# A gated recurrence feeding a mixture of experts on one core: another order table, and masks ahead of one state

## The chip, the core and the metric

The kernel runs on one core of a Trainium2 chip. Its engines are TensorE (PE; PEld is its weight load), VectorE (DVE), ScalarE (ACT), GpSimd (POOL) and SyncE (SP), which here only issues DMAs. Each engine works through its own list of instructions strictly in order and waits at an instruction until what that instruction needs is there. The metric is the device time of one execution in microseconds (us), as the median of several runs.

## The reference, cut to what matters

Four batches of eight heads, 768 steps, head size 48. A complex gate `a` of magnitude at most 0.999 drives a 48 x 48 state per head:

```
S = a[t] * S + k[t] v[t]^T        (complex; a scales the rows)
y[t] = q[t] . real(S)
x = y as 3072 tokens of 384
e = argmax(x @ w_gate);  g = softmax(x @ w_gate)[e]
out = g * relu(x @ w1[e]) @ w2[e]     (8 experts, 1024 wide, capacity 768)
```

## The kernel before, in words

**Tiling of the recurrence.** The 768 steps are cut into 8 chunks of 96. Inside a chunk the answer is an attention matrix with a triangular mask, and between chunks a state is handed on. What both need are the running products of the gate inside a chunk. VectorE computes these step by step (the scan, `scan_ops`, tiles `xy` and `near`) for two groups of two batches: group 0 is batches 0 and 1, group 1 is batches 2 and 3. Each group is done in seven pieces. For each piece a gate part runs ahead (`norm_ops`: tiles `a`, `xp`, `lnn`, `c0n`, `t5n`) and a product part behind (`post_ops`: tiles `qkin`, `wp`, `v0`, `qko`), at whose end GpSimd stores the scaled q and k to a scratch tensor in DRAM: the first 8 rows of each chunk to `scr0_0` or `scr1_0`, the other 88 to `scr0_1` or `scr1_1` (group 0 or 1).

**Units.** A unit is one batch and one chunk, named (batch, chunk). There are 32; the first 16 go (0,0), (1,0), (0,1), (1,1) up to (1,7), then (2,0) opens group 1. A unit (`Att.unit`) loads its part of the scratch (`qkc`, three buffers) and its values (`v`, three buffers), both issued by SyncE; TensorE turns q and k (`tr`), ScalarE copies them out (`qT`, `kT`); TensorE multiplies them in two halves (`pa`, one PSUM buffer in the first 14 units); VectorE masks each half into `a_sb`; TensorE forms the output (`y`). TensorE also forms the chunk's own state (`s`, one PSUM buffer shared with `y`), VectorE adds the state handed over (`s`), SyncE swaps its real and imaginary rows by two DMAs (`sx`), and the next state `z` comes from `u` (scaled `s`) and the scaled `sx`. The last chunk of a batch hands nothing on. ScalarE copies `y` to `xt`, TensorE turns it (`x`), and the router starts from that.

**What sets the order.** In slots, one per unit, each step has a place: the lists `SLOT`, `SLOT_A`, `SLOT_B` give the steps of a slot in order, each with the distance of the unit that it belongs to. `M0` and `M1` are the two masks, `D` is the state's sum and its swapping transfer, `U`, `ZA` and `ZB` make the next state, `A0` and `A1` are the two products, `T0` to `T3` the turns. `SLOT_A` is used for slot 13 alone. The slots up to 12 are mixed with the scan of group 1 into one list of 740 steps, and the table `ORDER` of 740 numbers says in which order these steps are issued on all of the engines. That part, from about 122 to 250 us, is called the stretch here; its table ends with the work of unit (0,6), the 13th. Behind it come slot 13 and the slots after it, in the order of their lists. After the last unit the expert part follows, with TensorE at work to the end.

The places that matter below: the transfer of a state is `swap` (L603 and L604), the mask is `cut` (L578), the state's three steps are L615, L620 and L625, the scratch loads are `load_qk` (L552), the value loads `load_v` (L555), the scratch stores L489 and L494, the turns L563, the two products L574.

Of the kernel before, what the change touches and what calls it, by code (L numbers as in the profile page):

```python
# [49 lines left out]
SLOT_A = SLOT[:-1] + [("LS", 3), SLOT[-1]]  # L50
SLOT_A.insert(SLOT_A.index(("D", 0)), ("LB", 3))
SLOT_A.remove(("L", 3))
SLOT_0 = SLOT[:1] + [("L", 2)] + SLOT[1:]
SLOT_B = [("S", 0), ("L", 3), ("R2", -3), ("G", -3), ("M0", -1), ("T1", 1), ("M1", -1), ("R3", -3), ("P", -3), ("W", -3),
          ("F", -2), ("X", -2), ("E", -2), ("D", 0), ("R1", -2), ("A0", 0), ("ZA", -1), ("T2", 1), ("Y", -1), ("T0", 1), ("A1", 0),
# [15 lines left out]
for j in SIDE:  # L71
# [5 lines left out]

ALONE = 14
ORDER = [
# [31 lines left out]
]  # L111
CAP = 0.9990000128746033

# [19 lines left out]
class Att:  # L133
# [520 lines left out]
    def slots(self):  # L654
# [8 lines left out]
        for n in range(-2, len(us) + 3):  # L663
            for i, (t, o) in enumerate(SLOT_0 if n == -2 else SLOT if n < ALONE - 1 else SLOT_A if n < ALONE else SLOT_D if n == len(us) - 2 else SLOT_B):
                if 0 <= n + o < len(us) and (t, o, n) != ("M0", -1, ALONE):
# [971 lines left out]
```

## Time and profile before

| what | value |
|---|---|
| median of 3 runs | 628.46 us (626.43 to 633.83) |
| the profiled execution's own time | 631.67 us |
| its span, first to last instruction | 630.0 us |
| PE, DVE, ACT, POOL busy | 87%, 70%, 55%, 33% of the span |
| mean granted TensorE clock | 0.951 |

The busy shares of the page are means over stages with different limits, so the stages are shown one by one below. Times in the rows are counted from the span's start. A row of the order of time gives the start, the duration, the line, what it writes and reads, how many instructions were merged in it, and in brackets how long the engine stood idle before it and what ended that. A granted clock of 1.00 is 2.4 GHz, 0.50 is 1.2 GHz.

### The profile page before, as it was taken

The numbers are of one execution on the slowest core, as the hardware profiler recorded it, in microseconds if no ns is written. First come the engines' busy times: TensorE is split into PE (matmuls) and PEld (weight loads), VectorE is DVE, ScalarE is ACT, GpSimd is POOL, SyncE is SP. The second block draws the span as 40 slices with busy tenths as digits, with TensorE's granted clock in tenths as the row PEclk, the third lists the DMA queues.
The fourth block names the chain that finished last, engine by engine and source line by source line (L and its number), as shares of the span: only waits on it lengthen the run. The fifth ranks groups of instructions, "written<-read, shape, count | busy, mean of one in ns | idle before, by whom it ended". The sixth has DMA issues, their size and how long they took to land.

```text
span 630.0 us, 12176 instructions
## 1 busy us (share of the span) xinstructions
PE 547.1 (87%) x4295; PEld 476.9 (76%) x4295; DVE 441.0 (70%) x1266; ACT 345.6 (55%) x771; POOL 207.7 (33%) x212
## 2 busy tenths in 40 slices
PE   0767656569899999799999998999999999999996
PEld 0333323247688889699889997998999999999995
DVE  5989999988999997249459786265555564556551
ACT  7777757787888785355454552243435353435440
POOL 9476863248878701004232221001010102020112
PEclk9887888688999999799999997999999999999999
DMA  6195858769888769568888821744546453636301
GB/s 201 51 295 207 274 187 286 247 208 230 256 251 234 192 204 260 149 141 227 216 207 212 212 76 48 238 120 131 163 121 178 132 168 119 179 114 188 107 27 49
DMA packets 73398, 111.88 MB, mean 178 GB/s; under 512 B 6568, under 2 KB 63214, under 8 KB 72048
## 3 DMA queue, kind: packets, MB, share of 16 engines
q1 hardware_dynamic: 66384, 77.13, 45.2%
q0 software_dynamic: 6944, 33.88, 15.3%
q8 instruction: 36, 0.59, 0.4%
q14 instruction: 34, 0.28, 0.1%
HBM read 72.99 MB, written 34.21 MB: 170 GB/s over the span
## 4 chain that ended last, share of the span: by engine, by line
PE 59%; DMA 10%; DVE 5%; ACT 4%; issue 1%; SPq 1%; POOLq 0%; POOL 0%; DVEq 0%; ACTq 0%
PE ph L1231 17%; PE my L1239 15%; PE pa L574 4%; PE tr L563 4%; PE s L587 4%; PE y L635 2%; PE x L844 2%; PE my L1253 2%; PE y L640 2%; DMA raw<-in_moe_w_dram 2%; PE wp L210 2%; PE yt L1193 1%; DMA qkc<-scr 1%; DMA scr<-qko 1%; DMA v<-in_v_dram 1%; PE mt L1167 1%
## 5 line engine op out<-in xcount | busy, mean ns | idle before, releaser
L1204 POOL DMA_INDIRECT out_dram<-o,xr x26 | 25.2, 969 | 156.7 <-DVE o L1203 139.9
L1277 ACT ACTIVATE hh<-ph 128x448 fp32r<-128x448 f32 (+5 forms) x64 | 33.0, 516 | 78.2 <-PE ph L1231 78.1
L1278 DVE SCALAR_TENSOR_TENSOR hl<-ph,hh 128x448 fp32r<-128x448 f32 (+5 forms) x64 | 37.3, 583 | 50.5 <-ACT hh L1277 49.1
L867 POOL DMA_INDIRECT disp<-x,idx x32 | 30.7, 960 | 119.3 <-DVE sl L929 41.9
L1129 DVE TENSOR_TENSOR lo<-raw,hi 128x384 fp32r<-128x384 f32 (+2 forms) x128 | 66.0, 551 | 3.2 <-ACT hi L1126 3.2
L210 PE MATMUL wp<-qko,ident 128*128 128x384 f32 x92 | 43.4, 623 | 27.3 <-ACT qko L408 23.5
L563 PE MATMUL tr<-ident,qkc 96*96 96x96 f32 x512 | 63.5, 252 | 3.8 <-DMA qkc<-scr 3.2
L574 PE MATMUL pa<-qT,kT 128*96 128x96 f32 x512 | 56.9, 255 | 5.8 <-DVE a_sb L578 5.5
L1126 ACT CAST hi<-raw 128x384 fp32r<-128x384 f32 (+2 forms) x128 | 60.0, 515 | 0.0
L1239 PE MATMUL my<-hh,lo 128*128 128x448 f32 (+5 forms) x168 | 59.6, 355 | 0.0
L1239 PE MATMUL my<-hl,hi 128*128 128x448 f32 (+5 forms) x168 | 59.2, 352 | 0.0
L210 PE MATMUL xp<-a,ident 128*128 128x384 f32 x84 | 37.8, 591 | 23.6 <-ACT a L238 23.1
L574 PEld LDWEIGHTS pa<-qT,kT 128*96 128x96 f32 x512 | 50.4, 170 | 8.5 <-DVE a_sb L578 5.9
L563 PEld LDWEIGHTS tr<-ident,qkc 96*96 96x96 f32 x512 | 47.8, 129 | 10.1 <-issue 4.1
L210 PEld LDWEIGHTS wp<-qko,ident 128*128 128x128 f32 x92 | 21.0, 241 | 45.2 <-ACT qko L408 31.8
L1239 PE MATMUL my<-hh,hi 128*128 128x448 f32 (+5 forms) x168 | 54.2, 355 | 0.0
L1231 PE MATMUL ph<-xh,hi 128*128 128x448 f32 (+5 forms) x192 | 49.9, 362 | 0.0
L336 DVE TENSOR_TENSOR xy<-a,near 128x192 f32<-128x192 f32 x135 | 47.4, 351 | 3.2
L1231 PE MATMUL ph<-xl,hi 128*128 128x448 f32 (+5 forms) x192 | 48.9, 354 | 0.0
L367 DVE TENSOR_REDUCE near<-xy 128x96 f32<-128x192 f32 x129 | 45.9, 356 | 4.3 <-ACT a L377 1.2
L568 ACT COPY qT<-tr 96x384 f32<-96x384 f32 x64 | 30.4, 476 | 32.0 <-PE tr L563 24.9
L210 PEld LDWEIGHTS xp<-a,ident 128*128 128x128 f32 x84 | 18.5, 231 | 38.3 <-issue 23.2
(220 smaller groups left out, 1362.3 us busy)
## 6 DMA issues: line engine op xcount, KB each, us to landing
raw<-in_moe_w_dram SPq DMA_DIRECT2D x64, 384.0 KB
qkc<-scr SPq DMA_DIRECT2D x32, 528.0 KB
scr<-qko POOLq DMA_DIRECT2D x10, 1536.0 KB
disp<-fill POOLq DMA_DIRECT2D x7, 772.0 KB
v<-in_v_dram SPq DMA_DIRECT2D x32, 144.0 KB
xr<-disp SPq DMA_DIRECT2D x6, 675.5 KB
sx<-s SPq DMA_DIRECT2D x56, 72.0 KB
a<-in_a_re_dram SPq DMA_DIRECT2D x10, 384.0 KB
```

Of the source, the lines that this page charges most:

```text
L210: nc.tensor.matmul(out=pt[:, :m], lhsT=self.ident, rhs=t[:, h:h + m], start=i == 0, stop=i == 1)
L336: nc.vector.tensor_tensor(out=xy, in0=crossed(a4[:, s, 1, cs]), in1=w, op=ALU.mult)
L367: nc.vector.tensor_reduce(out=o, in_=xy.rearrange("p z d -> p (z d)").rearrange("p (u d z) -> p u d z", u=2, z=2)[:, :, cs], op=ALU.add, a ...
L563: nc.tensor.transpose(out=pt[:, h * C:h * C + C], in_=qk(slice(0, C), 4 * hh + h, slice(z_ * C, z_ * C + C)), identity=self.ident[:C, :C])
L574: nc.tensor.matmul(out=pa[:, h * C:h * C + C], lhsT=kT[:, 4 * hh + h], rhs=qT[:, 4 * hh + h], start=True, stop=True)
L867: ins = nc.gpsimd.indirect_dma_start(out=self.disp, out_offset=bass.IndirectOffsetOnAxis(ap=idx[:, c:c + 1], axis=0), in_=x[:, c, :], in_o ...
L1126: nc.scalar.copy(out=hi[i][:, s], in_=raw[i][:, s])
L1129: nc.vector.tensor_tensor(out=lo[i][:, s], in0=raw[i][:, s], in1=hi[i][:, s].bitcast(F32), op=ALU.subtract)
L1231: nc.tensor.matmul(out=ph[:, :WIDTHS[e]], lhsT=a[:, k, fs], rhs=r[:, k, :WIDTHS[e]], start=k == 0 and i == 0, stop=k == KT - 1 and i == 2)
L1239: nc.tensor.matmul(out=py[m][:, :WIDTHS[e]], lhsT=a[:, f % self.PF, ms], rhs=r[:, :WIDTHS[e]], start=f == 0 and i == 0, stop=f == NF - 1 a ...
L1277: nc.scalar.activation(hh[:, :w], ph[:, :w], AF.Relu)
L1278: nc.vector.scalar_tensor_tensor(out=hl[:, :w], in0=ph[:, :w], scalar=0.0, in1=hh[:, :w].bitcast(F32), op0=ALU.max, op1=ALU.subtract)
```

## The change

The table `ORDER` is replaced by another one with the same 740 steps: some 170 of them stand elsewhere in the stretch, and near its end the transfer of the last state in it, that of unit (0,6), comes at an earlier place in SyncE's list. In `SLOT_A` the two steps `ZA` and `ZB` (of unit (0,6)) move behind the mask `M0` (of unit (1,6)). No instruction is added or removed.

```diff
 SLOT_A.remove(("L", 3))
+SLOT_A = [x for x in SLOT_A if x[0] not in ("ZA", "ZB")]
+for x in (("ZB", -1), ("ZA", -1)):
+    SLOT_A.insert(SLOT_A.index(("M0", 0)) + 1, x)
 SLOT_0 = SLOT[:1] + [("L", 2)] + SLOT[1:]
...
 ORDER = [
-    1, 0, 2, 6, 4, 9, 7, 5, 12, 11, 13, 14, 10, 17, 19, 3, 15, 21, 20, 29, 18, 23, 28, 36, 39, 104, 30, 26, 62, 27,
...
-    715, 719, 723, 729, 647, 732, 731, 726, 727, 735, 730, 733, 739, 712, 720, 734, 721, 728, 722,
+    1, 10, 0, 2, 6, 4, 9, 62, 5, 11, 104, 13, 3, 7, 14, 19, 21, 15, 23, 12, 17, 28, 29, 20, 18, 36, 39, 40, 8, 26, 27,
...
+    710, 717, 718, 726, 725, 729, 720, 732, 733, 681, 722, 727, 735, 730, 739, 728, 712, 731, 734,
 ]
```

In the lists below a line number of the kernel after the change is 3 higher than before. **SyncE at the end of the stretch**, first before, then with the change. The tiles are `sx_b_c` (swapped state of a unit), `v` and `qkc` (the three buffers each of values and scratch); `qkc0` is for unit (1,7), `qkc1` from `scr1` for unit (2,0).

```order
L603 DMA sx_1_5_2593<-s_1_5_2592 48x384
L604 DMA sx_1_5_2593<-s_1_5_2592 48x384
L555 DMA v1_106<-in_v_dram 96x384
L555 DMA v2_107<-in_v_dram 96x384
L552 DMA qkc0_102<-scr0_1_95 88x8x192
L552 DMA qkc0_102<-scr0_0_94 8x8x192
L603 DMA sx_0_6_2723<-s_0_6_2722 48x384
L604 DMA sx_0_6_2723<-s_0_6_2722 48x384
L552 DMA qkc1_103<-scr1_1_97 88x8x192
L603 DMA sx_1_6_2831<-s_1_6_2830 48x384
```

```order
L606 DMA sx_1_5_2569<-s_1_5_2568 48x384
L607 DMA sx_1_5_2569<-s_1_5_2568 48x384
L555 DMA qkc2_104<-scr0_1_95 88x8x192
L555 DMA qkc2_104<-scr0_0_94 8x8x192
L558 DMA v1_106<-in_v_dram 96x384
L606 DMA sx_0_6_2705<-s_0_6_2704 48x384
L607 DMA sx_0_6_2705<-s_0_6_2704 48x384
L558 DMA v2_107<-in_v_dram 96x384
L555 DMA qkc0_102<-scr0_1_95 88x8x192
L555 DMA qkc0_102<-scr0_0_94 8x8x192
L555 DMA qkc1_103<-scr1_1_97 88x8x192
L606 DMA sx_1_6_2831<-s_1_6_2830 48x384
```

The two DMAs of `sx_0_6` stood behind the load of `v2` and both loads of `qkc0`, and now stand ahead of them. The stores move too, on **GpSimd's queue at the same place**, before and with the change:

```order
L481 TENSOR_TENSOR qko_1_4_2089<-a4_1_4_1373,v0_1_4_2118 128x16x96
L489 DMA scr1_1_97<-qko_1_4_2089 128x3072
L620 TENSOR_TENSOR sx_1_3_2125<-sx_1_3_2125,pcol0_100 96x384
L625 TENSOR_TENSOR z2_117<-u_1_3_2238,sx_1_3_2125 96x384
L494 DMA scr1_0_96<-qko_1_6_2499 64x1536 x2
L489 DMA scr1_1_97<-qko_1_5_2363 128x3072
```

```order
L623 TENSOR_TENSOR sx_1_3_2126<-sx_1_3_2126,pcol0_100 96x384
L628 TENSOR_TENSOR z2_117<-u_1_3_2228,sx_1_3_2126 96x384
L484 TENSOR_TENSOR qko_1_4_2096<-a4_1_4_1355,v0_1_4_2131 128x16x96
L492 DMA scr1_1_97<-qko_1_4_2096 128x3072
L492 DMA scr1_1_97<-qko_1_5_2362 128x3072
L497 DMA scr1_0_96<-qko_1_6_2533 64x1536 x2
```

The store of `qko_1_5` now stands ahead of the two of `qko_1_6`, where it stood behind them. On VectorE the product that completes `qko_1_6` (L439 before) moves behind the sum of `s_0_6`, so these two stores come after it.

**VectorE behind the stretch**, slot 13 and the start of slot 14, before and with the change (`a_sb1` are the masked halves of unit (1,6), `sx_0_6`, `z1` and `u` belong to the states):

```order
L578 TENSOR_TENSOR a_sb0_113<-pa_0_6_1_2775,mask_81 96x384
L599 TENSOR_TENSOR s_1_6_2830<-s_1_6_2806,z2_117 96x384
L620 TENSOR_TENSOR sx_0_6_2723<-sx_0_6_2723,pcol0_100 96x384
L625 TENSOR_TENSOR z1_116<-u_0_6_2741,sx_0_6_2723 96x384
L578 TENSOR_TENSOR a_sb1_114<-pa_1_6_0_2837,mask_81 96x384
L615 TENSOR_TENSOR u_1_6_2874<-s_1_6_2830,pcol0_100 96x384
L578 TENSOR_TENSOR a_sb1_114<-pa_1_6_1_2882,mask_81 96x384
L620 TENSOR_TENSOR sx_1_6_2831<-sx_1_6_2831,pcol0_100 96x384
```

```order
L581 TENSOR_TENSOR a_sb0_113<-pa_0_6_1_2779,mask_81 96x384
L602 TENSOR_TENSOR s_1_6_2830<-s_1_6_2806,z2_117 96x384
L581 TENSOR_TENSOR a_sb1_114<-pa_1_6_0_2835,mask_81 96x384
L623 TENSOR_TENSOR sx_0_6_2705<-sx_0_6_2705,pcol0_100 96x384
L628 TENSOR_TENSOR z1_116<-u_0_6_2777,sx_0_6_2705 96x384
L618 TENSOR_TENSOR u_1_6_2874<-s_1_6_2830,pcol0_100 96x384
L581 TENSOR_TENSOR a_sb1_114<-pa_1_6_1_2882,mask_81 96x384
L623 TENSOR_TENSOR sx_1_6_2831<-sx_1_6_2831,pcol0_100 96x384
```

The first mask of unit (1,6) stood behind `sx_0_6` and `z1`, which wait for the transfer, and now stands ahead of them; the second mask stays behind.

**SyncE in the first part of the stretch**, before and with the change (`qkc0`, `qkc1`, `qkc2` for units (0,0), (1,0), (0,1); `qkin_1_1` are q and k for the second piece of group 1, `a_1_4` the gate of its fifth):

```order
L552 DMA qkc0_102<-scr0_1_95 88x8x192
L552 DMA qkc0_102<-scr0_0_94 8x8x192
L396 DMA qkin_1_1_1109<-in_q_dram 128x768
L397 DMA qkin_1_1_1109<-in_k_dram 128x768
L552 DMA qkc1_103<-scr0_1_95 88x8x192
L552 DMA qkc1_103<-scr0_0_94 8x8x192
L603 DMA sx_0_0_1232<-s_0_0_1231 48x384
L604 DMA sx_0_0_1232<-s_0_0_1231 48x384
L552 DMA qkc2_104<-scr0_1_95 88x8x192
L552 DMA qkc2_104<-scr0_0_94 8x8x192
L228 DMA a_1_4_1312<-in_a_re_dram 128x768
L229 DMA a_1_4_1312<-in_a_im_dram 128x768
```

```order
L555 DMA qkc0_102<-scr0_1_95 88x8x192
L555 DMA qkc0_102<-scr0_0_94 8x8x192
L555 DMA qkc1_103<-scr0_1_95 88x8x192
L555 DMA qkc1_103<-scr0_0_94 8x8x192
L399 DMA qkin_1_1_1132<-in_q_dram 128x768
L400 DMA qkin_1_1_1132<-in_k_dram 128x768
L555 DMA qkc2_104<-scr0_1_95 88x8x192
L555 DMA qkc2_104<-scr0_0_94 8x8x192
L606 DMA sx_0_0_1227<-s_0_0_1226 48x384
L607 DMA sx_0_0_1227<-s_0_0_1226 48x384
L558 DMA v2_107<-in_v_dram 96x384
L231 DMA a_1_4_1281<-in_a_re_dram 128x768
```

The loads of `qkc1` stand ahead of `qkin_1_1`, and those of `qkc2` ahead of the transfer `sx_0_0`, which waits for the first unit's state.

## Rows read from the trace of the kernel before

**Rows 1.** Stages of core 0: length, busy PE, PEld, DVE, ACT, POOL, PEclk, DMA, GB/s

```profile
140.67:145.67 5.00, 5.00 (x41) 5.00 (x41) 4.80 (x14) 4.70 (x9) 3.51 (x2) 0.66 0.65 153
170.00:226.00 56.00, 54.01 (x599) 45.92 (x597) 52.80 (x153) 44.92 (x109) 39.88 (x30) 1.00 0.82 235
226.00:255.00 29.00, 28.64 (x375) 26.44 (x372) 21.85 (x43) 18.38 (x57) 2.20 (x4) 1.00 0.78 210
259.26:264.73 5.47, 5.47 (x33) 5.22 (x33) 2.52 (x5) 1.03 (x3) 0.00 (x0) 0.50 0.51 133
```

**Rows 2.** TensorE in order of time, 251 to 268: start, us, line [idle before]

```profile
251.09 0.88 PE L844 MATMUL x<-wx,xt 112*96 112x104 f32 x8
...
251.80 0.84 PE L574 MATMUL pa<-qT,kT 128*96 128x96 f32 x8
...
252.48 0.49 PE L563 MATMUL tr<-ident,qkc 96*96 96x96 f32 x4
...
254.38 0.87 PE L563 MATMUL tr<-ident,qkc 96*96 96x96 f32 x8
...
259.26 1.59 PE L574 MATMUL pa<-qT,kT 128*96 128x96 f32 x8 [4.01 <-DVE a_sb L578]
...
267.38 0.82 PE L563 MATMUL tr<-ident,qkc 96*96 96x96 f32 x8
```

**Rows 3.** VectorE in order of time, 238 to 259

```profile
238.43 0.95 DVE L439 TENSOR_TENSOR qko<-a,qkin 128x768 f32<-128x768 f32 x1
...
244.53 0.54 DVE L599 TENSOR_TENSOR s<-s,z 96x384 f32<-96x384 f32 x1
...
246.80 0.56 DVE L620 TENSOR_TENSOR sx<-sx,pcol 96x384 f32<-96x384 f32 x1 [0.16 <-DMA sx<-s]
...
257.59 0.55 DVE L620 TENSOR_TENSOR sx<-sx,pcol 96x384 f32<-96x384 f32 x1 [6.08 <-DMA sx<-s]
...
258.65 0.55 DVE L578 TENSOR_TENSOR a_sb<-pa,mask 96x384 f32<-96x384 f32 x1
```

**Rows 4.** SyncE's DMA issues in order of time, 239 to 254

```profile
239.21 0.58 SPq L604 DMA_DIRECT2D sx<-s  x1
...
240.20 8.20 SPq L555 DMA_DIRECT2D v<-in_v_dram  x2
...
248.45 2.53 SPq L552 DMA_DIRECT2D qkc<-scr  x2
...
251.08 0.98 SPq L603 DMA_DIRECT2D sx<-s  x1
...
253.89 0.29 SPq L552 DMA_DIRECT2D qkc<-scr  x1
```

**Rows 5.** GpSimd's DMA issues in order of time, 241 to 244

```profile
241.60 1.12 POOL L494 DMA_DIRECT2D scr<-qko  x2 [22.38 <-DVE qko L481]
243.27 0.55 POOL L489 DMA_DIRECT2D scr<-qko  x1 [0.55 <-DVE psq L518]
```

**Rows 6.** Chain that ended last, in order of time: start, us, what

```profile
123.00 8.31 DMA scr<-qko
...
131.33 2.36 DMA qkc<-scr
...
190.93 6.50 DMA qkc<-scr
```

**Rows 7.** TensorE in order of time, at 140

```profile
140.67 0.84 PE L563 MATMUL tr<-ident,qkc 96*96 96x96 f32 x8 [1.90 <-DMA qkc<-scr]
```

**Rows 8.** VectorE in order of time, 137 to 149

```profile
137.01 0.36 DVE L367 TENSOR_REDUCE near<-xy 128x96 f32<-128x192 f32 x1 [1.21 <-ACT a L377]
...
148.41 0.57 DVE L448 TENSOR_TENSOR wp<-wp,v 128x384 f32<-128x384 f32 x1 [1.67 <-ACT v L430]
```

**Rows 9.** ScalarE in order of time, at 139

```profile
139.49 0.46 ACT L597 COPY s<-s 96x384 f32<-96x384 f32 x1
```

**Rows 10.** SyncE's DMA issues in order of time, at 132

```profile
132.59 0.88 SPq L552 DMA_DIRECT2D qkc<-scr  x2
```

58 rows, old and new, of the table ORDER are left out of this document.

## The prediction, on record before the change was run

> **What bounds the kernel now.** I read the views in this order: the table of stages, TensorE's and VectorE's order of time where a stage has idle time, then the issues of SyncE and GpSimd that these waits lead to.
>
> The stages [rows 1] show two different limits. From 170 to 226 us TensorE is busy 54.01 of 56.00 us and VectorE 52.80: nothing can be moved there to gain much. From 226 to 255 TensorE has 28.64 of 29.00, VectorE only 21.85: TensorE bounds, and VectorE has slack. Right behind, TensorE stands still for 4.01 us, from 255.25 to 259.26, for a mask `a_sb`, and its clock is then at 0.50 (1.2 GHz, against 2.4 GHz before the idle time) for 5.47 us [rows 1, 2]. After 265 it is at work again with only small gaps, into the expert part; so what is saved at 255 should reach the end.
>
> Why the mask is late is in VectorE's rows [rows 3]. It had stood idle for 6.08 us at the product `sx` at 257.59, waiting for a transfer; the mask of 258.65 is two instructions behind, though its input, the product `pa` of 251.80 + 0.84 = 252.64 [rows 2], had long been there. And the transfer is late because of SyncE [rows 4]: the state that it carries was complete at 244.53 + 0.54 = 245.07 [rows 3], but SyncE stood 8.20 us at the `v` loads of 240.20, then issued `qkc` from 248.45, and the transfer's second DMA only at 252.10. It landed 5.5 us later. A wait of VectorE, ended by a DMA that was queued 6 us after its data existed, is what the edit takes aim at.
>
> **The end of the stretch, step by step.** (1) The transfer. Its earlier place lets it go at about 245.1. The one before it took from 239.21 [rows 4] to 246.80 [rows 3], 7.6 us, the late one 257.59 - 251.08 = 6.5. So it lands at 251.6 to 252.7. The mask cannot start before 252.64, so the transfer is no longer what VectorE waits for. (2) The mask ahead of `sx` and `z1`. With the transfer at 245.1 this makes little difference by itself; it takes the mask out of the transfer's reach should that be late. `sx`, `z1` and `u` behind it cost 0.59, 0.47 and 0.47 start to start, so the second mask is free to go at 255, before TensorE asks for it. (3) TensorE then goes on at 255.25, the full 4.01 us earlier. (4) With no idle time I expect the clock to stay at 1.00: 5.47 us of work at half the clock is 2.74 at the full one, a further 2.74. Together 6.75.
>
> What may be given back. SyncE now stands at the transfer until 245.1, with `v2`, `qkc0` and `qkc1` queued behind. In the trace `v2` was held to 248.4 anyway by the buffer that it needs, so the transfer's early place costs them nothing as long as the sum of `s_0_6` comes before that. `qkc0`, still issued from 248.45, is wanted one product after 255.25, at 255.25 + 0.68 = 255.93 (0.68 is the start-to-start of `pa`, 251.80 to 252.48). Loads of this kind took 2.36 and 6.50 us [rows 6] and 140.67 - 132.59 = 8.08 [rows 7, 10]: it lands between 250.8 and 256.5, a wait of 0 to 0.6. `qkc1` needs the stores of GpSimd. The last product of `qko_1_6` (0.95, as at 238.43 [rows 3]) now follows the sum of `s_0_6`: 245.07 + 0.95, and 0.3 to the issue, is 246.3, against 241.60 before [rows 5]. A store took 8.31 [rows 6], and the one of 243.27 had landed when SyncE issued the load behind it, at 253.89 [rows 4, 5], 10.6 later. So the store lands at 254.6 to 256.9, the small load behind it at 257.0 to 263.4. TensorE wants it halfway through the turns of 267.38 [rows 2], at 267.82 - 6.75 = 261.07: a wait of 0 to 2.3. Both together 0 to 2.9. I take 0.6, since three of the four corners of the second give nothing or next to it. **End: 6.75 - 0.6 = 6.1.**
>
> **The first part of the stretch.** The other places of the table touch three waits. The copy of `near` by ScalarE held VectorE 1.21 us at 137.01, and the copy of `v` 1.67 at 148.41 [rows 8]. The load of unit (1,0) held TensorE 1.90 us at 140.67 [rows 7], and its clock over the next 5.00 us averaged 0.66 [rows 1], 1.70 lost. The load now goes ahead of two others, and ScalarE's copy is asked for earlier. But ScalarE's copy of `s_0_0` (139.49 to 139.95 [rows 9]) comes about 0.7 later, since two more small copies stand ahead of it, and the next state's product on TensorE needs the buffer that it frees. So TensorE's wait shrinks from 1.90 to perhaps 1.2 rather than to nothing, and the 1.21 of VectorE goes.
>
> What reaches 226 is the smaller of the two engines' gains, since both are nearly full from 170 on. Upper end: VectorE's 1.21 + 1.67 = 2.9 (TensorE's would be 3.6). Lower end: the other table could open one new wait of the size of the largest that VectorE had here, -1.7. The totals of work are the same, and I find as many pairs of neighbouring VectorE instructions of the scan that depend on each other as before. I take **1.5**, half of the upper end, since one of the two waits of VectorE is clearly addressed and the other is not.
>
> **Sum.** 6.1 + 1.5 = 7.6 on the profiled execution's own 631.67 (span 630.0 and 1.67 around it): 624.1. This execution is 3.2 above the median of 628.46, inside the spread of the three runs. Nothing in the terms hangs on that, so I take 7.6 off the median: **620.9**.
>
> **A rule that speaks against step (1).** In the trace a transfer that was issued at 239.21 was seen complete by 246.80, before the stores of 241.60 and 243.27 had landed, and the late one of 251.08 was seen after them. Neither shows what a transfer does that is issued between such stores. The Trainium skill, "DMA: Bandwidth & Descriptors", section "Queues, rings and completion order", says that a transfer's completion signal lands only after every earlier write from the same DMA engine, across its queues. By it a transfer issued among stores would be seen only when these are through. The sum would then be 7.1 instead of 7.6, for the reason given in rival R, whose numbers come from the rows.
>
> **The rivals.**
> - **A, the end alone.** The stretch gains nothing, its places cancel. For it: from 170 on both engines are full, and ScalarE's copy of `s_0_0` comes later. 628.46 - 6.1 = 622.4. Chance 0.17.
> - **B, the wait moves on.** The end gives back its upper 2.9 at the loads `qkc0` and `qkc1`, and the stretch gains nothing: 6.75 - 2.9 = 3.85, or 624.6; with the clock falling again after that wait it could be 627. For it: the store goes 4.7 us later than before. Against: half of the combinations of flights leave no wait. Chance 0.13.
> - **R, the transfer is seen with the stores.** If it lands at 256.9, the first mask is safe by its new place, but the second goes at 256.9 + 0.59 + 0.47 + 0.47 = 258.4 and ends at 259.0. TensorE wants it for `y` at 255.25 + 0.68 + 0.44 + 0.71 + 0.68 + 0.44 = 258.2, so it waits 0.5 to 0.8: 7.6 - 0.5 = 7.1, or 621.4. Chance 0.06.
> - **C, slower: the sum of `s_0_6` comes late.** SyncE stands at the transfer, and `v2`, both `qkc0` and `qkc1` queue behind; the stores of `qko_1_6` wait behind the same sum. It decides at about 247: a sum later than that by x shifts the store and the load by x. With 3 us, which a stretch that reads worse on VectorE would bring, the load lands at up to 266.4 against 261.07: 5.3 of waiting and again some 2.7 of clock, 8.0 lost beside the 6.75 gained, and the 3 us of the stretch itself: 628.46 + 8.0 - 6.75 + 3 = 632.7; between 630 and 636. For it: 170 steps in a stretch with no slack. Against: the sum is as many instructions from the end of VectorE's list as before. Chance 0.12.
> - **D, no effect.** The transfer is held by something that I don't see, and the first mask's new place alone only moves TensorE's wait from the first mask to the second: 627 to 629. Chance 0.09.
>
> **The numbers.** My forecast has 0.43, its own range 618 to 622.3. A difference of 1% of the median, 6.3 us, is about what a measurement of this kernel can tell from no change: below 622.2 is faster, above 634.7 slower. Faster: 0.38 of the forecast, 0.07 of A, 0.05 of R, 0.50. Slower: some 0.07, half of C and what it stands for. The rest, 0.43, is within 1%. The range goes from 617 (6.75 + 2.9 and 2 for the spread of the medians) to 629, with C and a tail of each side left out.
>
> **What would show it.** Right: no wait of TensorE over 1 us between 254 and 266, granted clock 1.00 there; the transfer's DMAs issued within 1 us of the sum of `s_0_6`; the wait of 137.01 gone. Wrong: a wait of TensorE at a `tr` near 256 or 261 ended by `qkc` (B); the second mask waiting at `sx` (R or D); the sum of `s_0_6` later than 247 (C); a stage 134 to 226 that is no shorter (A).

## The result, and the profile after

The change makes the kernel faster: 629.3 us before, 623.7 with it (medians of 20 runs each), ratio 0.9914 with a 95% interval of 0.9889 to 0.9939, which is 5.4 us less (3.8 to 7.0). The profiled execution has a span of 625.5 us against 630.0, 4.5 less. The kernel with both end edits and the new first part, tested below, was profiled in one of its slow runs (631.46 us, the median of its fast ones is 624.84), so its pieces stand in no comparison. (The table has 728 numbers for its 740 steps; the same 12 are left out before and after. By a plain count 692 of the 728 stand at another place in it, 191 of them by ten places or more, where "some 170" was said above. Line numbers with the change are 3 higher.)

TensorE with the change, in order of time (start, duration, line, what; in brackets the idle time before and what ended it):

```profile
255.87 0.87 PE L566 MATMUL tr<-ident,qkc 96*96 96x96 f32 x8
256.57 0.84 PE L577 MATMUL pa<-qT,kT 128*96 128x96 f32 x8
258.11 0.51 PE L566 MATMUL tr<-ident,qkc 96*96 96x96 f32 x4 [0.69 <-DMA qkc<-scr]
...
262.80 0.84 PE L566 MATMUL tr<-ident,qkc 96*96 96x96 f32 x8
```

These answer to the rows from 254.38 on in [rows 2]. The product `pa` follows the turns without a wait; the 4.01 us are gone. From these turns to the ones that were at 267.38 it is 262.80 - 255.87 = 6.93 us now, and was 267.38 - 254.38 = 13.00: 6.07 less. What is left is a wait of 0.69 for the load of unit (1,7). The stage has its full clock (length, then busy PE, PEld, DVE, ACT, POOL, the granted clock, DMA share, GB/s):

```profile
256.57:263.64 7.07, 6.37 (x86) 5.77 (x84) 1.96 (x4) 3.40 (x9) 0.00 (x0) 1.00 0.77 207
```

VectorE there with the change, beside [rows 3]:

```profile
245.78 0.55 DVE L602 TENSOR_TENSOR s<-s,z 96x384 f32<-96x384 f32 x1
...
254.17 0.55 DVE L581 TENSOR_TENSOR a_sb<-pa,mask 96x384 f32<-96x384 f32 x1 [1.17 <-PE pa L577]
254.65 0.54 DVE L623 TENSOR_TENSOR sx<-sx,pcol 96x384 f32<-96x384 f32 x1
...
257.45 0.55 DVE L581 TENSOR_TENSOR a_sb<-pa,mask 96x384 f32<-96x384 f32 x1 [1.20 <-PE pa L577]
```

The mask now waits for its own input, and `sx` behind it no longer waits at all. SyncE's issues, beside [rows 4], show why:

```profile
238.81 2.29 SPq L555 DMA_DIRECT2D qkc<-scr  x2
241.93 0.33 SPq L558 DMA_DIRECT2D v<-in_v_dram  x1
246.36 0.52 SPq L606 DMA_DIRECT2D sx<-s  x1
246.93 0.65 SPq L607 DMA_DIRECT2D sx<-s  x1
249.29 0.34 SPq L558 DMA_DIRECT2D v<-in_v_dram  x1
249.68 3.04 SPq L555 DMA_DIRECT2D qkc<-scr  x3
```

The transfer goes 0.03 us after the sum is complete (245.78 + 0.55 = 246.33), where it went 6 us after it before. The second `v` behind it still goes at about the same point, when its buffer is free.

But the sum itself is 1.25 us later than in [rows 3], and the end of the stretch with it (the turns of 255.87 by 1.49). The reason lies ahead of the change. The first product of the stretch, which both kernels reach through the same work, opens 3.08 us later in this execution, at 131.26 against 128.18; with both counted from there, the turns at the end come after 124.61 us with the change and 126.20 before, 1.59 less. TensorE in the first part of the stretch with the change:

```profile
131.26 2.90 PE L213 MATMUL wp<-qko,ident 128*128 128x384 f32 x4 [4.07 <-DVE t5n L278]
...
140.39 0.89 PE L577 MATMUL pa<-qT,kT 128*96 128x96 f32 x8 [0.66 <-ACT qT L571]
...
142.81 1.60 PE L590 MATMUL s<-v,qkc 128*96 128x96 f32 x16 [0.87 <-ACT s L600]
...
250.84 1.57 PE L590 MATMUL s<-v,qkc 128*96 128x96 f32 x16 [0.40 <-DMA v<-in_v_dram]
```

The wait of 1.90 for the load [rows 7] is gone, and 0.66 + 0.87 took its place, the second of them at `s` behind ScalarE's copy. A new wait of 0.40 for `v` stands at 250.84.

So this pair of traces alone would say: 6.1 at the end, 1.6 in the stretch, 7.7 together, less 3.1 by the chance of a later opening. One execution each is thin for a difference of 1.6, and that was the first thing to test.

### The profile page after: what moved, and what is told of

It reads as the page before. It is cut to its first block, busy times and chain, and to the rows that moved or that the text cites. A ratio compares the mean times of both kernels' runs of the same rounds, so it can differ in the third digit from the quotient of the medians.

```text
span 625.5 us, 12179 instructions
## 1 busy us (share of the span) xinstructions
PE 544.3 (87%) x4295; PEld 473.1 (76%) x4295; DVE 440.9 (70%) x1266; ACT 344.0 (55%) x771; POOL 208.0 (33%) x212
## 4 chain that ended last, share of the span: by engine, by line
PE 67%; DVE 11%; ACT 9%; DMA 9%; issue 2%; SPq 1%; POOLq 0%; POOL 0%; DVEq 0%; ACTq 0%
PE ph L1234 18%; PE my L1242 15%; PE wp L213 5%; PE tr L566 4%; PE pa L577 4%; PE s L590 4%; DMA v<-in_v_dram 4%; PE x L847 3%; PE y L638 2%; DVE xy L339 2%; PE xp L213 2%; PE my L1256 2%; PE y L643 2%; DMA qkc<-scr 2%; DMA a<-in_a_im_dram 2%
## 5 line engine op out<-in xcount | busy, mean ns | idle before, releaser
L213 PE MATMUL wp<-qko,ident 128*128 128x384 f32 x92 | 46.8, 661 | 27.9 <-ACT qko L411 22.9
L566 PE MATMUL tr<-ident,qkc 96*96 96x96 f32 x512 | 61.9, 248 | 2.3 <-DMA qkc<-scr 0.9
L577 PE MATMUL pa<-qT,kT 128*96 128x96 f32 x512 | 54.6, 249 | 2.2 <-ACT qT L571 1.3
L577 PEld LDWEIGHTS pa<-qT,kT 128*96 128x96 f32 x512 | 48.9, 164 | 4.6 <-issue 1.1
L590 PE MATMUL s<-v,qkc 128*96 128x96 f32 x448 | 43.3, 249 | 5.4 <-DMA v<-in_v_dram 4.1
L1234 PE MATMUL ph<-xh,lo 128*128 128x448 f32 (+5 forms) x192 | 47.1, 353 | 0.0
```

Source lines behind the costliest of these rows:

```text
L213: nc.tensor.matmul(out=pt[:, :m], lhsT=self.ident, rhs=t[:, h:h + m], start=i == 0, stop=i == 1)
L566: nc.tensor.transpose(out=pt[:, h * C:h * C + C], in_=qk(slice(0, C), 4 * hh + h, slice(z_ * C, z_ * C + C)), identity=self.ident[:C, :C])
L577: nc.tensor.matmul(out=pa[:, h * C:h * C + C], lhsT=kT[:, 4 * hh + h], rhs=qT[:, 4 * hh + h], start=True, stop=True)
L590: nc.tensor.matmul(out=ps[:, h * D:h * D + C], lhsT=qk(slice(None), h, slice(C, 2 * C)), rhs=v[:, h * D:h * D + C], start=True, stop=True)
L1234: nc.tensor.matmul(out=ph[:, :WIDTHS[e]], lhsT=a[:, k, fs], rhs=r[:, k, :WIDTHS[e]], start=k == 0 and i == 0, stop=k == KT - 1 and i == 2)
```

## The experiments

**Each end edit alone, both, and both with the first part's new places.** The theory: the two edits at the end overlap, and the stretch adds its 1.5. The first kernel has the old table and only the new `SLOT_A`; the second the old `SLOT_A` and one number moved; the third both; the fourth both, and the first 230 numbers of the table in the new order.

```diff
 # second and third kernel: the old table, step 720 is the transfer, 735 the load of v, 712 of qkc0
-    727, 735, 730, 733, 739, 712, 720, 734, 721, 728, 722,
+    727, 720, 735, 730, 733, 739, 712, 734, 721, 728, 722,
```

> Old table (transfer of the state of unit (0,6) still issued at 251), only the first mask of unit (1,6) ahead of it on VectorE. Theory (overlap: each of the two edits alone takes away most of the wait): transfer lands at 257.5 as before, TensorE goes on at 255.25 and meets the second mask instead, which ends at 257.6 + 0.59 + 0.47 + 0.47 + 0.55 = 259.7 against 258.2 where it is wanted: about 1.5 us of waiting is left of 4.0, with little of the slow clock behind it; 4 to 5 us faster than before. Rival (the wait only moves from the first mask to the second, at the same end): within 1.5 us of before. Rival (parts add, the transfer's place is the larger): 2 us faster.

> Old table with one number moved: the transfer of the state of unit (0,6) ahead of the load of v for unit (0,7); VectorE's list as before, both masks behind sx and z1. Theory (overlap): transfer issued at about 245.2, lands by 252.7, sx and z1 are through by 253.7, the first mask is at most 1 us late and TensorE, which asks for its result at 255.25, does not wait; 5 to 6 us faster than before. Rival (a transfer is seen complete only when the stores issued around it are through, at 253.9): the first mask ends at 255.5, a wait of 0.3; 5 us faster. Rival (the transfer is slow when it goes ahead of the loads, lands at 256 or later): 2 us faster or less.

> Both edits at the end of the stretch, the rest of the table as before. Theory (the end gives 6.1 and the other places in the stretch 1.5): 5.5 to 6.5 us faster than before, 1 to 2 us slower than the whole change. Rival (the stretch's other places are worth nothing on average): the same as the whole change, 5.6 faster. Rival (the end is worth less than its own trace, the stretch more): 4 us faster or less.

> Both edits at the end, and of the other places in the table only those of its first 230 numbers (to about 163 us); behind that the old order. Theory (the stretch's gain arises in its first part, at VectorE's waits of 1.21 and 1.67 us and TensorE's of 1.90): 1.5 to 2.5 us shorter than the kernel with the end alone, as far as VectorE's product wp near 166, and it keeps at least as much as the whole change at 254. Rival (the first part's gain is eaten by the places behind it): as short as the kernel with the end alone at 254. Rival (no gain in the stretch): no difference at 166 either.

Measured against before: the mask alone 0.9914 (0.9884 to 0.9943), the transfer alone 0.9931 (0.9902 to 0.9959), both 0.9921 (0.9892 to 0.9950), both with the first part 0.9908 (0.9874 to 0.9942): 4.3 to 5.8 us less, each. Each edit alone does most of the work, as the overlap has it, and the two gains don't add. The four intervals overlap, so these times tell none of the four kernels from another. VectorE with the mask alone:

```profile
253.76 0.55 DVE L583 TENSOR_TENSOR a_sb<-pa,mask 96x384 f32<-96x384 f32 x1 [1.17 <-PE pa L579]
259.20 0.56 DVE L625 TENSOR_TENSOR sx<-sx,pcol 96x384 f32<-96x384 f32 x1 [4.89 <-DMA sx<-s]
...
260.74 0.55 DVE L583 TENSOR_TENSOR a_sb<-pa,mask 96x384 f32<-96x384 f32 x1
```

The transfer is as late as before and VectorE still stands 4.89 us for it, but now behind the first mask. TensorE in the same kernel does not wait for the second one:

```profile
255.46 0.86 PE L568 MATMUL tr<-ident,qkc 96*96 96x96 f32 x8
256.16 0.84 PE L579 MATMUL pa<-qT,kT 128*96 128x96 f32 x8
258.49 0.51 PE L568 MATMUL tr<-ident,qkc 96*96 96x96 f32 x4 [1.49 <-DMA qkc<-scr]
...
260.65 0.39 PE L640 MATMUL y<-a_sb,v 128*64 128x96 f32 x4
```

The second mask starts at 260.74 and is through at 261.29. `y` starts at 260.65 with the heads of the first half and so has no wait: the wait for the load had already cost the time that the second mask would have cost. So the 1.5 us that were expected at the second mask came, at another place. With the transfer alone, VectorE:

```profile
254.05 0.56 DVE L622 TENSOR_TENSOR sx<-sx,pcol 96x384 f32<-96x384 f32 x1 [2.28 <-DMA sx<-s]
...
255.11 0.55 DVE L580 TENSOR_TENSOR a_sb<-pa,mask 96x384 f32<-96x384 f32 x1
```

SyncE's issues in that kernel:

```profile
245.35 0.50 SPq L605 DMA_DIRECT2D sx<-s  x1
245.91 1.87 SPq L606 DMA_DIRECT2D sx<-s  x1
248.31 0.94 SPq L557 DMA_DIRECT2D v<-in_v_dram  x1
249.30 4.87 SPq L554 DMA_DIRECT2D qkc<-scr  x3
```

TensorE, in the same kernel:

```profile
255.71 0.92 PE L576 MATMUL pa<-qT,kT 128*96 128x96 f32 x8 [0.20 <-DVE a_sb L580]
258.16 0.51 PE L565 MATMUL tr<-ident,qkc 96*96 96x96 f32 x4 [1.53 <-DMA qkc<-scr]
```

The transfer was seen at 254.05, 8.7 us after its first issue, and just when the third of the three `qkc` issues, which waits for the stores of GpSimd, was through (249.30 + 4.87 = 254.17). In two other traces of the old table with the transfer moved (the end alone again, and the end with the load first, both below) `sx` also waited for it: it was seen 8.4 and 9.1 us after the first issue, each time within 0.3 us of that same load; in two more it was in place by 8.1 us. That is what rival R of the prediction had a transfer do. But another reading is as good: the issue of the second DMA took 1.87 us here against 0.58 and 0.61 in the trace of before, and from its end (247.78) the transfer took 6.27, between the 7.01 and the 4.88 of the two transfers there. Which of the two it is, no run tells. Either way the mask ends at 255.66, and TensorE waits 0.20; with both edits even that is covered.

**The change and the kernel before once more, the table without the new `SLOT_A`, and the load ahead of `v`.** The last edit moves step 712 ahead of 735 in the new table:

```diff
-    710, 717, 718, 726, 725, 729, 720, 732, 733, 681, 722, 727, 735, 730, 739, 728, 712, 731, 734,
+    710, 717, 718, 726, 725, 729, 720, 732, 733, 681, 722, 727, 712, 735, 730, 739, 728, 731, 734,
```

> The whole change once more. Theory (all of the gain lies at the end of the stretch; the stretch itself is worth nothing, the traces' 1.5 came from the other kernel's execution): 4.5 to 6 us faster than before, the same as the kernel with the end alone; 124.2 to 125 us from the product wp that opens the stretch (near 130) to the turns near 255, and about 7 us from there to the turns near 262. Rival (the stretch's places are worth 1.5): 1 to 2 us faster than the kernel with the end alone.

> The kernel before once more, for a second trace. Theory (the stretch is as long as with the change): 124.2 to 125 us from the product wp that opens the stretch to the turns near 254, not the 126.2 of the first trace, whose stretch opened 2 to 3 us earlier than in the five other traces; and 13 us from those turns to the ones near 267, with a wait of 4 us and the slow clock. Rival (the stretch is really longer there): 126 us again.

> The whole new table, but sx and z1 of unit (0,6) ahead of the first mask of (1,6) as before. The transfer goes at 246.4, the stores of qko_1_6 only at 247.5, behind it. Theory 1 (a transfer takes 6 to 8 us from its own issue): VectorE's sx product waits until 253 to 254.2, the first mask ends by 255.8, TensorE waits at most 0.3; 4.5 to 6 us faster than before. Theory 2 (it is seen complete only with the stores around it, at about 256): sx waits until 256, the first mask ends at 257.6 where TensorE wants it at 256.6, 1 us lost and more behind; 3.5 to 4.5 us faster.

> The whole change, and the load qkc0 for unit (1,7) ahead of the load of v for unit (0,7) on SyncE: it goes at 247.6 to 248 in place of 249.7. Theory (the wait of TensorE that is left near 258, 0.7 to 2.2 us in the traces with both edits, hangs on this load's place behind v, which waits for a buffer): the wait near 258 goes, 0.7 to 2 us faster than the whole change, 6 to 7.5 faster than before. Rival (the load is limited by the transfers around it and not by its issue): as fast as the whole change. Rival (the load slows the transfer of the state, which VectorE then waits for): as fast or 1 us slower.

The change again 0.9894 (0.9862 to 0.9927), before again 0.9999 (0.9968 to 1.0031), the table alone 0.9883 (0.9832 to 0.9934), the load first 0.9886 (0.9838 to 0.9933). TensorE in the second trace of before:

```profile
256.08 0.87 PE L563 MATMUL tr<-ident,qkc 96*96 96x96 f32 x8
262.62 1.60 PE L574 MATMUL pa<-qT,kT 128*96 128x96 f32 x8 [5.67 <-DVE a_sb L578]
...
270.17 0.83 PE L563 MATMUL tr<-ident,qkc 96*96 96x96 f32 x8
```

The wait is there again, 5.67 this time, and the piece takes 270.17 - 256.08 = 14.09. And its stretch, opened at 131.07, is 125.01 long, within 0.4 of the change's 124.61: the first pair's 1.59 was not a fixed difference. With the table alone, VectorE's `sx` finds its transfer in place as soon as the sum ahead of it is done:

```profile
249.62 0.55 DVE L620 TENSOR_TENSOR sx<-sx,pcol 96x384 f32<-96x384 f32 x1
...
250.87 0.55 DVE L578 TENSOR_TENSOR a_sb<-pa,mask 96x384 f32<-96x384 f32 x1
```

SyncE had issued it in that kernel at 243.20:

```profile
243.20 0.52 SPq L603 DMA_DIRECT2D sx<-s  x1
243.77 0.64 SPq L604 DMA_DIRECT2D sx<-s  x1
```

Seen by 249.62, at most 6.4 us after its first issue, with the second one out in 0.64: theory 1, and `SLOT_A` adds nothing to the new table. In this table the store of `qko_1_5` is 5 us ahead of its old place, and the stores of `qko_1_6` are issued behind the transfer; in the old one all three were issued 2 to 4 us ahead of it.

The load's earlier place was not settled by this pair, since 622.81 against 623.23 is no difference. It is taken up below.

**The end alone beside the change, and the load ahead of `v` on two more tables.** The third and fourth kernel have both edits at the end and the load ahead of `v`; the fourth also the new order of the first 230 numbers.

> The kernel with both edits at the end and the old places elsewhere, again, beside the whole change on the same chip. Theory (in the old table TensorE's wait for the load of unit (1,0) near 141 ends at a time that depends little on when the stretch opens; with the new places TensorE follows the opening, and an early one is kept): the turns of unit (1,0) start at 140.7 to 142.1 wherever the stretch opens, after a wait of 1.4 us or more; 4.5 to 5.5 us faster than before, 1 to 2 us slower than the whole change. Rival (the other places are worth nothing): within 0.5 us of the whole change.

> The whole change, beside the kernel with the end alone. Theory (the first part's places are worth 1 to 2 us on average): 5.5 to 7 us faster than before, 1 to 2 us faster than the end alone; no wait of TensorE for the load of unit (1,0), but about 0.9 at the product s behind ScalarE's copy of s_0_0. Rival (worth nothing): the same as the end alone.

> Both edits at the end on the old table, and the load for unit (1,7) ahead of the v load for unit (0,7) on SyncE. Theory (the wait of TensorE near 258, 0.8 in the trace with the end alone, goes as it did on the new table): 0.5 to 1 us faster than the end alone; 5.9 to 6.2 us from the turns near 255 to those near 261, in place of 7.0. Rival (on this table the stores stand nearer, and the load comes no earlier for going ahead): the same as the end alone.

> As the kernel with the end and the load first, with the new places in the first 230 numbers of the table and the old ones behind. Theory (the first part gains 1 to 2 us on average, the places behind it lose 0.4): the fastest of the four, 6.5 to 8 us faster than before, 1 to 2 us faster than the same with the old first part, and 0.5 to 1.5 faster than the whole change. Rival (the first part is worth nothing): the same as with the old first part.

The end alone 0.9924 (0.9891 to 0.9957), the change 0.9908 (0.9877 to 0.9939), the end with the load first 0.9920 (0.9884 to 0.9955), the same with the new first part 0.9885 (0.9837 to 0.9932). The stretch opens early in all four traces. TensorE with the end alone (old places):

```profile
128.01 2.90 PE L215 MATMUL wp<-qko,ident 128*128 128x384 f32 x4 [3.84 <-DVE t5n L280]
...
139.47 0.84 PE L568 MATMUL tr<-ident,qkc 96*96 96x96 f32 x8 [2.31 <-DMA qkc<-scr]
...
147.44 0.51 PE L568 MATMUL tr<-ident,qkc 96*96 96x96 f32 x4 [1.49 <-DMA qkc<-scr]
```

and with the change:

```profile
128.56 2.83 PE L213 MATMUL wp<-qko,ident 128*128 128x384 f32 x4 [4.08 <-DVE t5n L278]
...
137.67 0.89 PE L577 MATMUL pa<-qT,kT 128*96 128x96 f32 x8 [0.66 <-ACT qT L571]
...
140.10 1.60 PE L590 MATMUL s<-v,qkc 128*96 128x96 f32 x16 [0.88 <-ACT s L600]
...
249.32 1.57 PE L590 MATMUL s<-v,qkc 128*96 128x96 f32 x16 [1.22 <-DMA v<-in_v_dram]
```

With the old places TensorE waits for two loads, 2.31 and 1.49; with the new ones for neither. But at 249.32 the change waits 1.22 for `v`. By time the end alone gives 4.8 us here and the change 5.8, with intervals that overlap, so the times don't show that the other places are worth anything. The load first, at last, did not help in time: with it on the old table the wait for that very load was the longest of those with both edits and the old places,

```profile
259.75 0.51 PE L568 MATMUL tr<-ident,qkc 96*96 96x96 f32 x4 [2.09 <-DMA qkc<-scr]
```

and it was 0.68 in the fourth kernel, and none in the one trace with the whole change. Without the edit it was none to 1.69 in the traces. So the place of its issue isn't shown to be what the load hangs on, and the rival fits better; what it does hang on stays open.

**All traces in one table.** Pieces in us: to the product `wp` of VectorE near 166, from there to the turns near 255, from those to the next eight turns near 262, and the rest of the span. "New" and "old" are the places in the first part and behind it.

| kernel | opens at | first part | middle | end | rest |
|---|---|---|---|---|---|
| before (old, old) | 128.18 | 37.72 | 88.48 | 13.00 | 362.6 |
| before again (old, old) | 131.07 | 36.05 | 88.96 | 14.09 | 358.5 |
| mask alone (old, old) | 130.08 | 36.90 | 88.48 | 7.74 | 359.2 |
| transfer alone (old, old) | 130.12 | 36.03 | 88.49 | 8.21 | 358.9 |
| end alone (old, old) | 131.13 | 35.92 | 88.48 | 7.03 | 363.0 |
| end alone again (old, old) | 128.01 | 36.71 | 88.48 | 7.29 | 358.8 |
| end, load first (old, old) | 128.37 | 38.64 | 89.10 | 8.32 | 358.7 |
| end, load first (new, old) | 128.19 | 35.53 | 88.61 | 6.92 | 359.6 |
| the change (new, new) | 131.26 | 35.74 | 88.87 | 6.93 | 362.7 |
| the change again | 130.33 | 35.87 | 89.14 | 6.97 | 359.4 |
| the change, third | 128.56 | 36.08 | 89.71 | 6.17 | 362.7 |
| table alone (new, new) | 128.58 | 35.23 | 88.76 | 7.92 | 362.2 |
| load first (new, new) | 128.55 | 35.67 | 89.48 | 6.05 | 363.0 |

The end: 13.00 and 14.09 before, 6.17 to 6.97 in the three traces of the change, 6.9 less on average. The first part: 36.85 in the mean of seven with the old places, 35.69 in the mean of six with the new ones, 1.2 less. The middle: 88.63 in eight against 89.19 in five, 0.6 more, by the wait for `v` of unit (1,6): it is 0.25 to 1.22 us in the five traces, and without it each of their middles is 88.5, as most of the old ones are. By the traces the stretch as a whole is worth about 0.6, and it's worth most where it opens early: with an opening before 129 the old places take 36.7 to 38.6, with one after 130 35.9 to 36.9, and the new ones 35.2 to 36.1 either way.

## Why the prediction was right, and where it was off

The sign, the mechanism of the end and the range held: 623.7 lies in 617 to 629, and the interval excludes no change. It lies outside the forecast's own 618 to 622.3, though, nearest to the rivals A (622.4) and B (624.6), and in the class "within 1%" that had 0.43. And 20 runs each tell more than the 1% that was allowed for: their interval is 1.6 us to either side. The predicted 620.9 was 2.8 too low, of which 0.8 lies in the starting point (the median of before was 628.46 of three runs and is 629.3 of twenty) and 2.0 in the gain, 7.6 forecast against 5.6 between the medians.

**The end: right, to the tenth in the first pair.** 6.1 was forecast and 6.07 came (6.9 over all traces, since the second one of before lost more). Step (3), the wait, and step (4), the clock, went as written. The give-back of 0.6 was a wait of 0.69 at the load `qkc0`, within its bounds up to a tenth, and none at unit (2,0): the late store of `qko_1_6` cost nothing (rival B's larger part), and the sum of `s_0_6` came at 246.33, ahead of the 247 at which rival C decides. Step (2) called the mask's new place of little worth by itself "with the transfer at 245.1"; on the new table that is so (the table alone is as fast), but on the old one it does most of the job alone, which the text did not price; rival D, by which that place alone only moves the wait, is refuted by the mask alone.

**Step (1) was too quick by one case.** "It lands at 251.6 to 252.7" held on the new table, at most 6.4 us from its issue. On the old table it was seen at 254.05. The two flights that it was built from were counted from different ends: 7.6 from the second DMA of a transfer (239.21), 6.5 from the first of another (251.08). In the trace of before, SyncE issued the first DMA of the earlier one here:

```profile
238.63 0.52 SPq L603 DMA_DIRECT2D sx<-s  x1
```

From it that transfer took 246.80 - 238.63 = 8.17, near the 8.4 to 9.1 of the old table with the transfer moved. That row, too, was of a transfer issued before the stores; the one in question came behind them. The rule that was weighed, of the Trainium skill's "DMA: Bandwidth & Descriptors", "Queues, rings and completion order", says that a completion signal lands only after every earlier write of the same DMA engine. It agrees with that trace (seen at 254.05, the load that waits for the stores out by 254.17), but no run here separates it from the slower issue of the second DMA, or from mere crowding of the engines. Its price was 0.20 of TensorE's time where it showed.

**The stretch: the right size in one pair by luck, too large on average.** Forecast 1.5, shown 1.59 in the first pair, about 0.6 over all traces. The 1.90 did shrink to 0.66 + 0.87 as in the text, with the copy of `s_0_0` as what is late next. Two things were missed. The first is in "Nothing in the terms hangs on that": the 1.5 is half of VectorE's 1.21 + 1.67, and those two waits were that one execution's. With the change both are gone, but in the second trace of before, with the same order, the same two instructions read

```profile
139.50 0.36 DVE L367 TENSOR_REDUCE near<-xy 128x96 f32<-128x192 f32 x1 [0.47 <-ACT qT L568]
...
149.16 0.56 DVE L448 TENSOR_TENSOR wp<-wp,v 128x384 f32<-128x384 f32 x1
```

and the other five traces with the old places show the same 0.47 and none. The second is the load of `v1`, for unit (1,6). It goes when TensorE's `y` of the unit that had the buffer frees it, and the new order has that `y` nearer to the reader, the product `s`. Before, beside the issue at 240.20 [rows 4]:

```profile
239.99 0.34 PE L640 MATMUL y<-qT,z 128*48 128x96 f32 x4
...
249.32 1.60 PE L587 MATMUL s<-v,qkc 128*96 128x96 f32 x16
```

and with the change, beside the issue at 241.93:

```profile
241.72 0.34 PE L643 MATMUL y<-qT,z 128*48 128x96 f32 x4
```

The load had 249.32 - 240.20 = 9.12 us, and has 8.51 to the time at which `s` could start without its wait (250.84 - 0.40 - 241.93). The two `qkc2` loads that now stand ahead of it on SyncE were out at 241.10 and did not hold it in this trace; in the third trace of the change they held it some 0.4 more. TensorE's wait at `s` that follows, a term that the prediction left out, takes back half.

**What stays open.** The pieces sum to 6.9 + 0.6 = 7.5 us, the timed runs say 5.4, 6.7 and 5.8. The rest of the span comes in two sizes, near 359 and near 363, in both kernels, and 4 of 5 traces with the new middle have the long one against 2 of 8 with the old. With five and eight traces that may be chance. If it is not, the new table gives about 2 us back later (0.80 - 0.25 = 0.55 of the 3.7 between the means of the two sizes). Part of it can be placed: between 265 and 345 us TensorE waits 1.9 to 3.7 us in all at `s` for `v` loads in four of the six long ones (before, the change, the table alone, the load first), and at most 0.31 in each of the short ones. What makes these loads late, and the other two long, is open. The kernel with the new first part and the old middle has the shortest trace of all, 618.8, and 0.9885 against the change's 0.9908 beside it; the intervals overlap, so it's a candidate and not a shown improvement.

## What to carry to other kernels

When a wait ends with a DMA, look at when its data existed and what stood ahead of its issue; moving the issue and moving the waiting instruction are two cures of one wait, worth the same once and not twice. A cost read from one profile holds for that execution: mark where a stage opens in several traces before a stall of 2 us in it is taken for a property of the kernel. A load goes when its buffer is free: where products change places, price the time that is left between the one that frees a buffer and the reader of the load into it. And count the flight of a transfer of two DMAs from the same one of them each time.

## What the runs showed of the hardware

The opening of the stretch varies by 3 us between executions of the same work, 128.0 to 131.3, and TensorE's granted clock goes with it. The windows view from 85 to 112 us of the kernel before, which opened at 128.18:

```profile
85.00:112.00 27.00, 18.77 (x44) 8.62 (x42) 25.52 (x80) 16.83 (x33) 11.26 (x10) 0.89 0.71 244
```

and with the change, which opened at 131.26:

```profile
85.00:112.00 27.00, 19.45 (x36) 8.98 (x36) 23.58 (x79) 15.01 (x29) 11.49 (x11) 0.72 0.64 223
```

In the other traces it was 0.84 to 0.89 at openings of 128.01 to 128.58, 0.79 to 0.80 at 130.08 to 130.33, and 0.72 at 131.07 to 131.17. VectorE's wait of 1.94 us at 109.11 in the profile after ended with an instruction of ScalarE, which itself had waited 0.81 us for TensorE's `wp` at 107.13. Whether the low clock makes the opening late, or both come from something earlier, is not shown. Not every wait brought the low clock: after the 1.49, 1.53 and 2.09 us above it was 1.00 (2.4 GHz) over the next 5.2 to 5.4 us, after 4.01 and 5.67 it was 0.50 and 0.58 over the next 5.5 and 5.4 (1.2 GHz for all or most of it). After 2.16 us, in the kernel with the end and the new first part, it was 0.67 over the next 5.2. The second term of the end, 2.74 us, hung on that.
